# Plain float32 products in the first chunk's first four d_ff blocks of an attention + FFN kernel on one core

## The chip, the cores and the metric

One NeuronCore of a Trainium2 chip. The metric is device microseconds of one execution. Five engines run their own instruction streams, each in the order in which the program was built: TensorE (PE, with its weight loads as PEld), VectorE (DVE), ScalarE (ACT), GpSimd (POOL) and SyncE (SP, which issues all DMAs here). An instruction waits for semaphores of others, and everything behind it on its engine waits with it.

## What is computed

Attention over a sliding window with four sink keys, and behind it an FFN:

```python
scores = 0.125 * q @ k.T                         # batch 4, 8 heads, seq 768, head 64
keep = (pos_k < n_sink) | (0 <= pos_q - pos_k < window)    # 4 sinks, window 128
a = softmax(where(keep, scores, -1e9));  x = (a @ v)       # as 3072 tokens x 512
h = x @ w_in                                     # 512 x 2048
g = where(h >= 1, h, where(h <= -1, 0, (h + 1) ** 2 / 4))
out = g @ w_out                                  # 2048 x 512, float32
```

## The kernel before

The 3072 tokens are cut into eight chunks of 384 tokens (`CT` = 3 tiles of 128), the four first halves of the batches ahead of the four second halves. A **unit** is one head of one chunk; there are 64. For each unit `attn_steps(n)` issues scores (PE, L249), the row maximum (DVE, L253), the exponential (ACT, L257), a sum on POOL (L262), its reciprocal (DVE, L263), the normalisation (L275 on ACT, L277 on DVE), transposes (PE, L326 to L328), their copies (ACT, L329, L333), and the product with v. Scores of unit n stand beside transposes of unit n-1, and the product of an older one.

The first 16 units (`NATIVE`, chunks 0 and 1) take their operands in float32 itself: the PE multiplies them as they are, and two heads share one product with v (`av2`, L369, copied to `xn` by L371). All other products are made of float32r parts: an operand is rounded to float32r, the rest is a second part, and a product is three matmuls (high by high, high by low, low by high). Rounding is a cast on ACT, the rest a subtraction on DVE or POOL.

The FFN goes over 16 blocks j of 128 d_ff columns. `stage1` makes a block of h (four slices `ct` of d_model, three matmuls each, L445), then relu, square (ACT, L452, L453), a min/max (DVE, L454), the cast `gh` (ACT, L455) and the rest `gl` (L456, on POOL for chunk 0, else on DVE). `stage2` (L464) multiplies it with w_out, two blocks later (`LAG`).

The weights come as 64-bit words, 32 tiles of 0.5 MB (w_in and w_out of each block in turn, n = 0 to 31). `weights(n)` fetches up to `AHEAD` = 3 tiles beyond n, and `decode` turns one into float32 with three bit operations on DVE (L157 to L159), then splits it: a cast on ACT (L160) and a subtraction on DVE (L161).

The loop over chunks builds a **stretch** at a time: `spread` merges the attention steps of one chunk with the steps of what is due beside it. The **first stretch** is the attention of chunk 0 (up to the scores of unit 9) with the first `WFIRST` = 13 weight tiles. The **second stretch** is the rest of chunk 1's attention with the FFN of chunk 0 and the other 19 tiles. The third has the FFN of chunk 1, and so on. PE's order is the order written here; the other engines' orders were set by a scheduler when the program was built. All fetches of the first two stretches stand in one queue on SP, in program order.

## Time and profile before

| | |
|---|---|
| median of 3 runs | 725.88 us (724.31 to 726.3) |
| the profiled execution | 726.5 us, its span 724.8 us |
| busy PE / PEld / DVE / ACT / POOL | 97% / 85% / 73% / 70% / 42% |
| mean granted PE clock | 0.992 |
| instructions | 12264 |

Busy shares are of the span. A matmul's record holds its time in the pipeline, so consecutive records overlap; what one costs is read from start to start. DVE's and ACT's records overlap too, by about a tenth of a microsecond. "A <- B" after an idle time names what ended the wait.

### The profile page before, as it was taken

Reading aid. Unit: us, or ns where it says so; the run is one execution under the profiler, and the core shown is the slowest. Engines: PE = TensorE matmul, PEld = TensorE weight load, DVE = VectorE, ACT = ScalarE, POOL = GpSimd, SP = SyncE. Lnnn points to the kernel's source line nnn. Section 1 sums busy time; section 2 is a strip of 40 time slices with the busy share of each in tenths; the row PEclk is TensorE's granted clock in tenths of the full one; section 3 lists DMA queues with packets and bytes.
Section 4 is the critical chain, followed back from the end, with each engine's and each line's share of the span. In section 5 each row is a group of like instructions: output and inputs, shape, how many; then the busy total and the mean of one; then the engine's idle time right before and its main releaser. Section 6 shows DMA issues by size and latency. Waiting matters only on the chain.

```text
span 724.8 us, 12264 instructions
## 1 busy us (share of the span) xinstructions
PE 699.7 (97%) x3841; PEld 615.6 (85%) x3841; DVE 529.4 (73%) x1393; ACT 504.4 (70%) x1313; POOL 305.7 (42%) x529
## 2 busy tenths in 40 slices
PE   6879999999999999999999999999999999999996
PEld 4547778899989999999889998999989989989895
DVE  8988989578786777687887887878877787833221
ACT  5887677687776777687677877778777867644432
POOL 3002224755453545455564666645556365500000
PEclk9989999999999999999999999999999999999999
DMA  7453453222221322153242533334323342101001
GB/s 291 146 225 127 188 193 121 58 89 58 57 57 33 96 65 66 46 186 114 88 125 64 170 126 115 115 103 137 122 82 127 107 125 74 67 1 44 0 1 48
DMA packets 38568, 73.54 MB, mean 101 GB/s; under 512 B 6752, under 2 KB 21088, under 8 KB 38496
## 3 DMA queue, kind: packets, MB, share of 16 engines
q1 hardware_dynamic: 38496, 72.68, 31.2%
q8 instruction: 32, 0.52, 0.3%
q14 instruction: 40, 0.33, 0.1%
HBM read 66.37 MB, written 6.29 MB: 100 GB/s over the span
## 4 chain that ended last, share of the span: by engine, by line
PE 70%; DVE 13%; ACT 6%; DMA 5%; POOL 3%; issue 2%; POOLq 0%; ACTq 0%; SPq 0%; DVEq 0%
PE h_ps L445 28%; PE o_ps L464 28%; PE ps_a L249 6%; PE ps_a L404 4%; ACT p L257 2%; PE ps_a L336 2%; DVE k_s L233 2%; DMA k_r<-qk 1%; DVE p L277 1%; PE ps_a L369 1%; PE ps_a L326 1%; DMA r<-vx 1%; DVE gl L456 1%; ACT k_s L231 1%; DMA r<-qk 1%
## 5 line engine op out<-in xcount | busy, mean ns | idle before, releaser
L445 PE MATMUL h_ps<-x,wi 128*128 128x384 f32 x1536 | 310.1, 340 | 0.0
L445 PEld LDWEIGHTS h_ps<-x,wi 128*128 128x128 f32 x1536 | 262.7, 188 | 10.8 <-issue 2.7
L464 PE MATMUL o_ps<-w,gh 128*128 128x512 f32 x768 | 243.6, 398 | 0.0
L464 PE MATMUL o_ps<-w,gl 128*128 128x512 f32 x384 | 150.9, 393 | 0.3 <-POOL gl L456 0.3
L464 PEld LDWEIGHTS o_ps<-w,gh 128*128 128x128 f32 x768 | 134.1, 188 | 15.8 <-issue 1.4
L454 DVE SCALAR_TENSOR_TENSOR g<-g,h_ps 128x384 f32<-128x384 f32 x128 | 70.2, 548 | 66.4 <-ACT g L453 65.5
L452 ACT ACTIVATE g<-h_ps,half 128x384 f32<-128x384 f32 x128 | 73.9, 577 | 62.0 <-PE h_ps L445 61.6
L257 ACT ACTIVATE p<-p,peak 128x260 f32<-128x260 f32 (+1 forms) x192 | 94.0, 490 | 30.7 <-DVE peak L253 29.2
L235 POOL TENSOR_TENSOR q_l<-r,q_h 128x384 fp32r<-128x384 f32 x48 | 50.4, 1049 | 131.9 <-ACT q_h L234 121.6
L455 ACT CAST gh<-g 128x384 fp32r<-128x384 f32 x128 | 65.5, 511 | 53.0 <-DVE g L454 52.1
L456 DVE TENSOR_TENSOR gl<-g,gh 128x384 fp32r<-128x384 f32 x112 | 70.2, 627 | 24.7 <-ACT gh L455 23.7
L464 PEld LDWEIGHTS o_ps<-w,gl 128*128 128x128 f32 x384 | 72.0, 188 | 18.2 <-POOL gl L456 0.8
L253 DVE CUSTOM_DVE_ANT_0 p<-ps_a,m 128x260 f32<-128x260 f32 (+1 forms) x176 | 68.2, 398 | 16.6 <-PE ps_a L249 15.9
L233 DVE TENSOR_TENSOR k_s<-k_r,k_s 64x524 fp32r<-64x524 f32 (+1 forms) x44 | 47.2, 1073 | 42.8 <-ACT k_s L231 42.7
L453 ACT ACTIVATE g<-g 128x384 f32<-128x384 f32 x128 | 67.0, 524 | 2.6
L348 POOL TENSOR_SCALAR_AFFINE_SELECT pt<-pt 128x384 fp32r<-128x384 f32 (+1 forms) x96 | 50.3, 525 | 23.8 <-DVE pt L341 21.8
L277 DVE TENSOR_SCALAR p<-p,stat 128x132 f32<-128x132 f32 (+1 forms) x160 | 56.8, 404 | 0.2
L262 POOL TENSOR_SCALAR stat<-stat 128x3 f32<-128x3 f32 x64 | 28.6, 447 | 66.1 <-ACT p L257 61.4
L346 POOL TENSOR_SCALAR_AFFINE_SELECT pt<-pt 128x384 fp32r<-128x384 f32 (+1 forms) x96 | 52.6, 549 | 6.9 <-ACT pt L340 2.7
L404 PEld LDWEIGHTS ps_a<-pt,v_s 128*128 128x128 f32 x304 | 46.5, 188 | 2.2
L404 PE MATMUL ps_a<-pt,v_s 128*128 128x256 f32 (+1 forms) x304 | 46.4, 272 | 0.0
L249 PE MATMUL ps_a<-k_s,q_h 128*128 128x260 f32 (+1 forms) x144 | 40.4, 281 | 4.4 <-DVE sk L343 3.1
(116 smaller groups left out, 986.1 us busy)
## 6 DMA issues: line engine op xcount, KB each, us to landing
r<-qk SPq DMA_DIRECT2D x48, 192.0 KB
k_r<-qk SPq DMA_DIRECT2D x32, 262.0 KB
w<-w_in SPq DMA_DIRECT2D x16, 512.0 KB
w<-w_out SPq DMA_DIRECT2D x16, 512.0 KB
again<-w_in SPq DMA_DIRECT2D x16, 512.0 KB
...
```

The source lines that it names most:

```text
L249: nc.tensor.matmul(ps[:, lo:260], lhsT=q[:, i * P:(i + 1) * P], rhs=k_s[:, c0:c0 + 260 - lo], start=(j == 0), stop=(j == len(qs) - 1))
L253: found = nc.vector.tensor_tensor_reduce(out=p[:, i, lo:260], in0=ps[:, lo:260], in1=m, scale=-0.125, scalar=3.0e38, op0=ALU.add, op1=ALU. ...
L257: nc.scalar.activation(p[:, i, lo:260], p[:, i, lo:260], AF.Exp, bias=peak_i, scale=-1.0, accum_out=stat[:, i:i + 1])
L277: (nc.gpsimd if eng == "p" else nc.vector).tensor_scalar(p[:, i, lo:260], p[:, i, lo:260], r, None, op0=ALU.mult)
L404: nc.tensor.matmul(z, lhsT=w, rhs=y, start=(n == 0), stop=(n == len(mms) - 1))
L445: nc.tensor.matmul(h_ps[:, :T], lhsT=w_i[j][:, w, ct * P:(ct + 1) * P], rhs=x[:, y, ct], start=(ct == 0 and n == 0), stop=(ct == NCT - 1 a ...
L452: nc.scalar.activation(g, h_ps[:, :T], AF.Relu, bias=half, scale=0.5)
L453: nc.scalar.activation(g, g, AF.Square)
L454: nc.vector.scalar_tensor_tensor(g, g, 1.0, h_ps[:, :T], op0=ALU.min, op1=ALU.max)
L455: nc.scalar.copy(gh, g)
L456: (nc.gpsimd if row0 == GL_POOL else nc.vector).tensor_tensor(gl, g, gh.bitcast(F32), op=ALU.subtract)
L464: nc.tensor.matmul(o_ps[tt], lhsT=gg[:, tt * P:(tt + 1) * P], rhs=w_o[j][:, w], start=(j == 0 and n == 0), stop=(j == NJ - 1 and n == 2))
```

## The change

In chunk 0, blocks 0 to 3 (`PLAIN` = 4) are multiplied as float32 itself: one plain matmul stands where three float32r matmuls stood, in both stages, on the decoded weights, on `xn` and on an unsplit `gh`. So the first eight weight tiles are decoded without cast and subtraction; `halves(j)` splits them later, in the stretch of chunk 1, whose FFN takes its blocks in the order 4 to 15, 0 to 3. The first stretch has 10 weight tiles instead of 13, the second 22. `gl` of chunk 0 (12 blocks now) goes to DVE. Of the three normalisations of a unit, chunk 0 keeps one on DVE and two on ACT, and chunk 1 has all three on ACT. All weight tiles come from one pool of 33 buffers (before: 16 constants and a pool of 16), three tiles are fetched ahead to the end, q's tiles have two buffers instead of three, and the later second reading of the weights uses the spare buffer.

```diff
 NATIVE = 16
+PLAIN = 4
-GL_POOL = 0
-NORM = "vaa"
+NORM = ("vaa", "aaa")
-WFIRST = 13
+WFIRST = 10
...
+    def decode(w, o, words):
         low, x = words[:, :, 0], words[:, :, 1]
+        nc.vector.tensor_scalar(o, x, 3, 0x3FFFFFFF, op0=ALU.logical_shift_left, op1=ALU.bitwise_and)
+        nc.vector.scalar_tensor_tensor(o, x, -0x40000000, o, op0=ALU.bitwise_and, op1=ALU.bitwise_or)
+        nc.vector.scalar_tensor_tensor(w, low, 29, o, op0=ALU.logical_shift_right, op1=ALU.bitwise_or)
+
+    def parts(t, w):
+        nc.scalar.copy(t[:, 0], w)
+        nc.vector.tensor_tensor(t[:, 1], w, t[:, 0].bitcast(F32), op=ALU.subtract)
+
+    def halves(j):
+        w = plain.pop(j).bitcast(F32)
+        with tc.issue_after(last_max[-1].ins):
+            for i in (0, 1):
+                t = (w_i, w_o)[i][j] = wpool.tile([P, 2, DM], F32R, name="w")
+                parts(t, w[:, i])
...
-        for deep, late, f in ((3, 4, load2), (2, 1, values2)):
+        for deep, late, f in ((2, 2, load2), (2, 1, values2)):
...
+        if j in plain:
+            nc.tensor.matmul(h_ps[:, :T], lhsT=plain[j][:, 0, cs].bitcast(F32), rhs=xn[:, ct],
+                             start=(ct == 0), stop=(ct == NCT - 1))
+        else:
+            for n, (w, y) in enumerate(((0, 0), (0, 1), (1, 0))):
+                nc.tensor.matmul(h_ps[:, :T], lhsT=w_i[j][:, w, cs], rhs=x[:, y, ct],
+                                 start=(ct == 0 and n == 0), stop=(ct == NCT - 1 and n == 2))
...
+        if j in plain:
+            gh = gh.bitcast(F32)
+            nc.vector.scalar_tensor_tensor(gh, g, 1.0, h_ps[:, :T], op0=ALU.min, op1=ALU.max)
+            hs[j] = gh, None
+            return
...
-        (nc.gpsimd if row0 == GL_POOL else nc.vector).tensor_tensor(gl, g, gh.bitcast(F32), op=ALU.subtract)
+        nc.vector.tensor_tensor(gl, g, gh.bitcast(F32), op=ALU.subtract)
...
+        if j in plain:
+            terms = [(gh, plain[j][:, 1].bitcast(F32))]
+        else:
+            terms = [(gh, w_o[j][:, 0]), (gh, w_o[j][:, 1]), (gl, w_o[j][:, 0])]
...
+        js = [(j + PLAIN * (c == 1)) % NJ for j in range(NJ)]
...
+            if c == 1 and n % 2 and n // 2 in range(1, PLAIN + 1):
+                steps.append((0.0, lambda j=n // 2 - 1: halves(j)))
```

**PE, where the second stretch begins**, before: scores of units 10 and 11 (ps_a<-qp) stand singly among blocks 0 to 2 of stage 1.

```order
L249 MATMUL ps_a<-qp 128x128
L445 MATMUL h_ps<-x,wi_151 128x384 x3
L249 MATMUL ps_a<-qp 128x260
L445 MATMUL h_ps<-x,wi_151 128x384 x9
L249 MATMUL ps_a<-qp 128x260
L445 MATMUL h_ps<-x,wi_152 128x384 x3
L326 MATMUL ps_a<-ident,p 128x128 x2
L328 MATMUL ps_a<-ident,p 4x128
L445 MATMUL h_ps<-x,wi_152 128x384 x9
```

The same place of the change (L266, L463 and L343 are the lines of these steps there; `w` is a decoded weight tile):

```order
L266 MATMUL ps_a<-qp 128x128
L463 MATMUL h_ps<-xn,w 128x384
L266 MATMUL ps_a<-qp 128x260
L463 MATMUL h_ps<-xn,w 128x384 x3
L266 MATMUL ps_a<-qp 128x260
L463 MATMUL h_ps<-xn,w 128x384
L343 MATMUL ps_a<-ident,p 128x128 x2
L345 MATMUL ps_a<-ident,p 4x128
L463 MATMUL h_ps<-xn,w 128x384 x2
```

Each group of three became one, and everything up to block 3 is of the plain kind, attention included. Over the whole second stretch a run of plain matmuls is followed by float32r ones 22 times before, and 14 times now.

**DVE, at the first weight tiles of the first stretch** (o and w: decode; ISA: the row maximum of a unit), before:

```order
L253 ISA p,peak<-ps_a,m1n 128x260
L253 ISA peak 128x1
L263 RECIPROCAL stat<-stat 128x3
L277 TENSOR_SCALAR p<-p,stat 128x128
L157 TENSOR_SCALAR o<-w 128x512
L253 ISA p,peak<-ps_a,m_106 128x260
L253 ISA peak 128x1
L158 SCALAR_TENSOR_TENSOR o<-w,o 128x512
```

The change at that place:

```order
L156 TENSOR_SCALAR o<-w 128x512
L157 SCALAR_TENSOR_TENSOR o<-w,o 128x512
L270 ISA p,peak<-ps_a,m1n 128x260
L270 ISA peak 128x1
L280 RECIPROCAL stat<-stat 128x3
L158 SCALAR_TENSOR_TENSOR w<-w,o 128x512
L270 ISA p,peak<-ps_a,m_106 128x260
L270 ISA peak 128x1
```

The first decode begins two operations ahead of unit 1's second maximum and ahead of unit 0's reciprocal; the subtractions that follow further down before (L161) are gone for the first eight tiles.

**DVE, in the middle of the second stretch** before (L454 is the min/max of a block):

```order
L253 ISA p,peak<-ps_a,m_109 128x128
L253 ISA peak 128x1
L157 TENSOR_SCALAR o<-w 128x512
L161 TENSOR_TENSOR wi_158<-o,wi_158 128x512
L253 ISA p,peak<-ps_a,m1n 128x260
L253 ISA peak 128x1
L158 SCALAR_TENSOR_TENSOR o<-w,o 128x512
L159 SCALAR_TENSOR_TENSOR o<-w,o 128x512
```

And of the change (L483 is gl):

```order
L270 ISA p,peak<-ps_a,m_109 128x128
L270 ISA peak 128x1
L158 SCALAR_TENSOR_TENSOR o<-w,o 128x512
L156 TENSOR_SCALAR o<-w 128x512
L270 ISA p,peak<-ps_a,m1n 128x260
L270 ISA peak 128x1
L483 TENSOR_TENSOR gl<-g,gh 128x384
L157 SCALAR_TENSOR_TENSOR o<-w,o 128x512
L162 TENSOR_TENSOR w<-o,w 128x512
```

A gl stands between the maxima and the decodes, where before POOL had it.

## Rows read from the trace of the kernel before

**Rows 1.** The page: the span, and PE's busy tenths in 40 slices of 18.1 us.

```profile
span 724.8 us, 12264 instructions
PE   6879999999999999999999999999999999999996
```

**Rows 2.** Busy time in the three stretches from one product of a pair of heads to the next (us from the start; length, then busy us and instructions of PE, PEld, DVE, ACT, POOL, granted clock, DMA share, GB/s), and their sum.

```profile
33.60:43.80 10.20, 7.89 (x43) 4.97 (x41) 9.35 (x29) 8.84 (x27) 0.71 (x2) 0.83 0.62 219
sum 30.60, PE 23.63 PEld 14.90 DVE 27.94 ACT 26.87 POOL 1.62; mean PE 7.88 PEld 4.97 DVE 9.31 ACT 8.96 POOL 0.54
```

**Rows 3.** PE's timeline over one of them (start, us, what; the idle time before and what ended it).

```profile
33.53 1.38 PE L249 MATMUL ps_a<-qp 64*128 64x128 f32 x6
34.85 0.44 PE L326 MATMUL ps_a<-ident,p 128*128 128x128 f32 x2
...
36.58 1.14 PE L249 MATMUL ps_a<-qp 64*128 64x260 f32 x4 [0.29 <-ACT spn L333]
39.58 0.80 PE L326 MATMUL ps_a<-ident,p 128*128 128x128 f32 x2 [1.86 <-ACT p L275]
...
41.16 2.40 PE L369 MATMUL ps_a<-pt,v_s 128*64 128x128 f32 x12
...
43.75 0.93 PE L249 MATMUL ps_a<-qp 64*128 64x128 f32 x4
```

**Rows 4.** Groups of instructions from 23.4 to 54 us, ACT and DVE: the parts of the weights' decoding (count | busy us, mean ns | idle before).

```profile
L160 ACT CAST wi<-o 128x512 fp32r<-128x512 f32 x5 | 3.1, 615 | 0.8 <-DVE o L159 0.7
L160 ACT CAST w<-o 128x512 fp32r<-128x512 f32 x5 | 3.1, 611 | 0.0
L158 DVE SCALAR_TENSOR_TENSOR o<-w,o 128x512 int32<-128x512 int32 x8 | 5.5, 684 | 0.0
L161 DVE TENSOR_TENSOR wi<-o,wi 128x512 fp32r<-128x512 f32 x5 | 3.4, 688 | 2.0 <-ACT wi L160 2.0
L157 DVE TENSOR_SCALAR o<-w 128x512 int32<-128x512 int32 x8 | 3.3, 418 | 0.0
```

**Rows 5.** Two stretches of the same time, as in rows 2: the granted clock is the third number from the end.

```profile
33.30:40.10 6.80, 4.49 (x26) 2.70 (x23) 6.62 (x24) 6.20 (x20) 0.23 (x1) 1.00 0.80 279
40.10:43.50 3.40, 3.40 (x19) 2.27 (x21) 3.03 (x7) 2.35 (x8) 0.49 (x1) 0.50 0.24 99
```

**Rows 6.** PE's timeline in the first 24 us.

```profile
12.96 2.52 PE L249 MATMUL ps_a<-qp 64*128 64x128 f32 x6
15.41 0.69 PE L326 MATMUL ps_a<-ident,p 128*128 128x128 f32 x2
...
23.34 0.93 PE L249 MATMUL ps_a<-qp 64*128 64x128 f32 x4
```

**Rows 7.** PE's timeline where the second stretch begins.

```profile
54.41 0.80 PE L445 MATMUL h_ps<-x,wi 128*128 128x384 f32 x3
55.14 0.70 PE L249 MATMUL ps_a<-qp 64*128 64x260 f32 x2
55.77 1.84 PE L445 MATMUL h_ps<-x,wi 128*128 128x384 f32 x9
57.54 0.70 PE L249 MATMUL ps_a<-qp 64*128 64x260 f32 x2
```

**Rows 8.** PE's timeline late in the second stretch, with no attention between.

```profile
135.25 2.25 PE L445 MATMUL h_ps<-x,wi 128*128 128x384 f32 x12
137.33 0.63 PE L464 MATMUL o_ps<-w,gh 128*128 128x512 f32 x2
...
139.41 2.25 PE L445 MATMUL h_ps<-x,wi 128*128 128x384 f32 x12
```

**Rows 9.** The second stretch: for whom PE waited from 54 to 146 us (us, times, longest), and busy time in two parts of it.

```profile
PE o_ps L464 <- POOL gl L456: 0.3, 1, 0.3
...
54.00:132.00 78.00, 77.71 (x421) 60.43 (x420) 70.79 (x160) 56.93 (x151) 26.04 (x28) 1.00 0.43 150
132.00:146.00 14.00, 13.67 (x69) 11.89 (x68) 5.26 (x12) 7.95 (x20) 8.35 (x13) 1.00 0.19 52
```

**Rows 10.** Groups of instructions from 54 to 132 us, DVE and POOL.

```profile
L158 DVE SCALAR_TENSOR_TENSOR o<-w,o 128x512 int32<-128x512 int32 x19 | 16.8, 884 | 0.2
L159 DVE SCALAR_TENSOR_TENSOR o<-w,o 128x512 int32<-128x512 int32 x19 | 15.2, 801 | 0.0
L157 DVE TENSOR_SCALAR o<-w 128x512 int32<-128x512 int32 x19 | 9.4, 493 | 2.3 <-DMA w<-w_in 2.3
L456 POOL TENSOR_TENSOR gl<-g,gh 128x384 fp32r<-128x384 f32 x12 | 14.3, 1192 | 31.8 <-ACT gh L455 18.5 <-issue 13.1
L235 POOL TENSOR_TENSOR q_l<-r,q_h 128x384 fp32r<-128x384 f32 x3 | 4.2, 1387 | 0.2
```

**Rows 11.** One DVE and one POOL instruction of the timelines at 86 us.

```profile
86.88 1.49 DVE L161 TENSOR_TENSOR wi<-o,wi 128x512 fp32r<-128x512 f32 x1
...
86.59 1.23 POOL L456 TENSOR_TENSOR gl<-g,gh 128x384 fp32r<-128x384 f32 x1 [3.80 <-issue]
```

**Rows 12.** DVE's timeline: the end of w_in's last tile.

```profile
124.59 0.68 DVE L161 TENSOR_TENSOR wi<-o,wi 128x512 fp32r<-128x512 f32 x1
```

**Rows 13.** The page's group of gl on DVE in the other chunks, and the busy time of the third stretch.

```profile
L456 DVE TENSOR_TENSOR gl<-g,gh 128x384 fp32r<-128x384 f32 x112 | 70.2, 627 | 24.7 <-ACT gh L455 23.7
...
146.00:230.00 84.00, 84.00 (x482) 76.86 (x481) 64.79 (x182) 60.93 (x169) 40.32 (x74) 1.00 0.21 59
```

More of the change, by code (lines that the diff above doesn't have):

```diff
@@ L137, in attn_ffn @@
         nc.gpsimd.memset(t, 0.0)
-    w_i = [const.tile([P, 2, DM], F32R, name=f"wi{j}") for j in range(NJ)]
-    w_o = [None] * NJ
-    raw = {}
+    w_i, w_o = [None] * NJ, [None] * NJ
+    raw, plain = {}, {}
     inorder = [True]
@@ L168, in f @@
             j, i = n // 2, n % 2
-            for k in range(n, min(n + min(AHEAD, NJ - n // 2 - 1) + 1, 2 * NJ)):
+            for k in range(n, min(n + AHEAD + 1, 2 * NJ)):
                 if k not in raw:
@@ L172, in f @@
                     fetch(raw[k], (w_in, w_out)[k % 2][k // 2].bitcast(I32))
-            words = raw[n].rearrange("p (c two) -> p c two", two=2)
-            if i:
-                w_o[j] = wpool.tile([P, 2, DM], F32R, name="w")
-            with tc.issue_after(last_max[-1].ins) if last_max else nullcontext():
-                decode((w_i, w_o)[i][j], moe.tile([P, DM], I32, name="o"), words)
+            words = raw.pop(n).rearrange("p (c two) -> p c two", two=2)
+            raw[n] = None
+            if j < PLAIN:
+                if not i:
+                    plain[j] = wpool.tile([P, 2, DM], I32, name="w")
+            else:
+                t = (w_i, w_o)[i][j] = wpool.tile([P, 2, DM], F32R, name="w")
+            o = moe.tile([P, DM], I32, name="o")
+            with tc.issue_after(last_max[-1].ins) if last_max else nullcontext():
+                if j < PLAIN:
+                    decode(plain[j][:, i], o, words)
+                else:
+                    decode(o, o, words)
+                    parts(t, o.bitcast(F32))
         return f
@@ L272, in scores @@
             r = stat[:, CT + i:CT + i + 1]
-            eng = NORM[i] if units.index(u) < NATIVE else "v"
+            eng = NORM[units.index(u) // H][i] if units.index(u) < NATIVE else "v"
             if eng == "a":
@@ L422, in attn_steps @@
         if n == 0:
-            steps = [steps[i] for i in (0, 3, 1, 4, 2)]
+            steps = [steps[i] for i in (0, 2, 1, 3)]
         if n + 1 >= NATIVE and -1 in us:
@@ L443, in stage1 @@
         h_ps = hs[j]
-        for n, (w, y) in enumerate(((0, 0), (0, 1), (1, 0))):
-            nc.tensor.matmul(h_ps[:, :T], lhsT=w_i[j][:, w, ct * P:(ct + 1) * P], rhs=x[:, y, ct],
-                             start=(ct == 0 and n == 0), stop=(ct == NCT - 1 and n == 2))
+        cs = slice(ct * P, (ct + 1) * P)
+        if j in plain:
+            nc.tensor.matmul(h_ps[:, :T], lhsT=plain[j][:, 0, cs].bitcast(F32), rhs=xn[:, ct],
+                             start=(ct == 0), stop=(ct == NCT - 1))
+        else:
+            for n, (w, y) in enumerate(((0, 0), (0, 1), (1, 0))):
+                nc.tensor.matmul(h_ps[:, :T], lhsT=w_i[j][:, w, cs], rhs=x[:, y, ct],
+                                 start=(ct == 0 and n == 0), stop=(ct == NCT - 1 and n == 2))
         if ct < NCT - 1:
@@ L512, in attn_ffn @@
     early = ExitStack()
-    first.append(early.enter_context(tc.tile_pool(name="first", bufs=3)))
+    first.append(early.enter_context(tc.tile_pool(name="first", bufs=2)))
     prev = wsteps[:WFIRST]
@@ L525, in attn_ffn @@
             early.close()
-            chk.append(fast.enter_context(tc.tile_pool(name="chk", bufs=2)))
-        prev = moe_steps(rows[c], tail)
+            chk += [fast.enter_context(tc.tile_pool(name=f"chk{i}", bufs=i)) for i in (2, 1)]
+        prev = moe_steps(rows[c], tail, c)
         if c == 0:
@@ L549, in attn_ffn @@
     nc.vector.tensor_copy(other, flag[0:1, 2:3])
-    for _, f in prev + tail:
+    for _, f in prev + sum(tail, []):
         f()
@@ L629, in attn_ffn @@
                     tail = []
-                    for _, f in moe_steps(b * S + t0 * P, tail) + tail:
+                    for _, f in moe_steps(b * S + t0 * P, tail) + sum(tail, []):
                         f()
```

55 lines of the change are left out of this document (27 added, 28 removed).

## The prediction

> **What bounds the kernel now.** I read the page first: PE is busy in nearly the whole span, except in the first three slices [rows 1]. So a change can win time in the first 54 us or by taking work off PE; it loses time wherever it gives PE work or lets it wait. Then I read the first stretch in pieces. From one product of a pair of heads to the next takes 10.2 us, three times over, and there DVE is busy 9.31 us in the mean and ACT 8.96, PE 7.88 [rows 2]. PE's row shows where the pair's time goes: scores and transposes are done early, PE then stands for 1.86 us until ACT's normalisation frees the transposes at 39.58, and from there transposes and the product take until 43.75, 4.17 us [rows 3]. That last piece is slow because the granted clock had fallen to half, 1.2 GHz, after the sparse time before it, while it had been whole, 2.4 GHz, from 33.3 to 40.1 [rows 5]. The three score matmuls of a unit (six records) take 1.32 us there [rows 3] and 2.45 us from 12.96 to 15.41 [rows 6]: before the first product, PE runs at the lower level as well and is busy back to back, so nothing on DVE can shorten that piece.
>
> From 54 us on PE is the bound. In the second stretch it waited for one thing that the profile shows, 0.3 us for gl on POOL [rows 9]. DVE was busy 70.79 of 78.0 us to 132 and 5.26 of 14.0 us behind it [rows 9], but ahead of its need: w_in's last tile was done at 125.3 [rows 12] and first used at 139.41 [rows 8].
>
> **The change, part by part.** The sum is made against the profiled execution, 726.5 us (span 724.8 and 1.7 around it), which lies 0.6 above the median of 725.88.
>
> *The start.* The first decode now stands with two operations ahead of unit 1's second maximum and unit 0's reciprocal, 0.42 and 0.68 us long [rows 4]. PE is back to back soon behind it, so the delay stays: +0.3 us, between 0 and the two operations' 1.1.
>
> *The wait ahead of the transposes.* In each of the three pairs two weight casts stand ahead of the awaited normalisation on ACT, 0.6 us each [rows 4], and they go for the plain tiles. Three bit operations per unit stay in DVE's queue ahead of the reciprocals. Out of 1.2 us at most and 0 at least I take 0.7 a pair: -2.1 us.
>
> *The clock.* At the whole clock the transposes and the product would take half of 4.17 us, 2.1. With a shorter period PE's idle time is a larger part shorter, but 1.2 us of the 1.86 remain; so the clock may fall in some pairs and not in others. I take 1.7 of three pairs: -3.4 us, with 0 and -6.2 as bounds. The floor below everything is ACT: 26.87 us less 6.2 us of casts [rows 2, 4] leave 6.9 us a pair, that is 9.9 us off the three.
>
> *Plain products.* A unit's scores, 128 + 2 x 260 = 648 columns, take 1.32 us [rows 3], 2.04 ns a column with their two ends; the product with v, of 128 rows and with two heads side by side, takes 2.59 us for 768 columns at half the clock [rows 3], which is 1.69 ns at the whole. The new matmuls are wide, so I take 1.69: 0.65 us for 384 columns and 0.86 for 512. Three float32r matmuls take 2.08/4 = 0.52 us in stage 1 and 2.08/3 = 0.69 in stage 2 [rows 8]. There are 16 of the first and 12 of the second: 16 x 0.13 + 12 x 0.17 = +4.1 us; with 2.04 it is +8.4.
>
> The Trainium skill gives another price: its page Perfetto Trace Analysis, section Engine Utilization, puts TensorE's output rate for FP32_LOW_HIGH at half the normal one, two cycles a column. By it the new matmuls would take 0.32 and 0.43 us, and this term would be 16 x -0.20 + 12 x -0.26 = -6.3 us. The rows do not bear it out: each plain matmul shows as two records, and the pair of them takes four cycles a column.
>
> *Changes of kind.* A plain 260-column matmul between float32r ones takes 0.63 us [rows 7] where 260 x 1.69 ns are 0.44, and the float32r matmuls between two plain ones take 0.73 for three and 1.77 for nine [rows 7], 0.21 more than 0.173 each. So each such round costs 0.40 us. The second stretch has 22 of them before and 14 now: -3.2 us. The lower bound for this gain is 0, if plain matmuls pay the same ends among themselves.
>
> *DVE in the second stretch.* Three more tiles: 3 x (0.42 + 2 x 0.68 + 0.69) = +7.4 us; twelve gl at 0.627 us [rows 13] = +7.5; eight normalisations of 128 columns fewer, each below the 0.42 us of a decode's first operation, which is four times as wide [rows 4], so between 0 and -3.4: I take -2.2. Against that stands what POOL's gl did: while it ran, a DVE subtraction took 1.49 us [rows 11] instead of 0.69 [rows 4]. L158, L159 and L157 took 884, 801 and 493 ns there against 684, some 680 and 418 before 54 us [rows 4, 10]: 19 x (0.20 + 0.12 + 0.075) = 7.5 us, of which POOL's gl, 14.3 of 18.5 us [rows 10], made 5.8. In all DVE has +6.9 us: 83.0 busy of the 92 us instead of 76.1. PE still bounds, with the 14.1 us of lead as its cover. I allow +1.0 us for waits behind a fuller DVE; if the cover is gone, see the rivals.
>
> *The rest.* PE's wait for gl on POOL goes: -0.3. The later splits are eight casts and eight subtractions, 4.9 and 5.5 us, in a stretch where PE never waited, DVE was busy 64.79 and ACT 60.93 of 84.0 us [rows 13]; ACT's third normalisation goes into the second stretch, where it was busy 56.93 of 78.0 [rows 9]. I put both at 0; uncovered, the splits would cost 5.5. The fetches still stand behind the wait for a pair's v buffer on SP, before and now, and q's third buffer goes; but q of a pair is then asked for two units ahead, and the DMAs were busy to 0.24 and 0.80 of their time in a pair's two halves [rows 5], so 0 here too, 1 at most.
>
> Sum: +0.3 - 2.1 - 3.4 + 4.1 - 3.2 + 1.0 - 0.3 = -3.6, so 722.9 for an execution like the profiled one and **722.3 us** beside the median.
>
> **The rivals.**
> *The clock stays whole in all three pairs.* For it: the period shrinks towards ACT's 6.9 us and PE's share rises. Against it: a wait of 1.2 us or so remains, and in the pair shown the clock fell behind a wait of 1.86 us. It gives 2.8 more: 719.5.
> *The clock falls in each pair as before.* For it: the same order of work, and the wait in the same place. Then the 3.4 us don't come: 725.7.
> *DVE becomes the bound of the second stretch: slower.* For it: it is nearly full to 132 us already. If POOL's other work (q_l) keeps delaying the decodes as gl did, DVE has 70.8 + 7.4 + 7.5 - 1.7 (six of the normalisations) = 84.0 us to do in the time to 132, with 7.2 idle as now 91.2, 13.2 too many. Behind 132 it has 8.7 us free; if half of that makes up for it, PE waits 8.8 us instead of 1.0: 730.1. The point from which it decides is where the maxima and gl come later than PE's next step, that is, when DVE's delay passes the 14.1 us by which the weights are early. Against it: gl is gone from POOL.
> *Plain matmuls pay ends,* 2.04 ns a column: 4.3 more, 726.6.
> *Plain matmuls need two cycles a column,* as if the array passed the operands only twice: 10.4 less, 711.9. This is what the rule of the Trainium skill's page above would do here.
>
> **How the numbers follow.** The forecast has 0.45, the whole clock 0.13, the lost clock 0.20, DVE 0.12, ends 0.08, two cycles 0.02. The measurement tells 0.3%, 2.2 us, from no change. The forecast's own range is 720 to 725; three quarters of it lie below 723.7. So faster is 0.33 + 0.13 + 0.02 and a little of the lost clock, 0.50; slower is nearly all of DVE, 0.11; the same 0.39. The range reaches from ACT's side, 718.5, to 728, where part of DVE's case is left out.
>
> **What would show it.** The product of the fourth pair ends at 54.0 now; I expect 48.8 (46 with the whole clock, 52 without any). The pairs' periods fall from 10.2 to 8 or 9 us, with the granted clock at half in one or two. Plain matmuls of stage 1 start 0.65 us apart, of stage 2 0.86. From the end of the first stretch to the start of chunk 1's FFN it should take 1 to 2 us longer than before, PE without waits over 0.5 us. DVE's decode operations of the second stretch come down towards 0.68 us. The forecast is wrong if PE waits there for DVE, or if the first stretch ends after 52.

## The result and the profile after

The changed kernel is slower: 735.17 us, median of 4 (732.56 to 735.56), beside 726.09 us (724.31 to 728.62) of the kernel before in the same comparison; ratio 1.0115, 95% interval 1.0076 to 1.0153. The forecast was 722.3 us in a range of 718.5 to 728. The profiled execution took 735.5 us, 9.0 more than that of before. From the page of after (40 slices of the span, busy tenths; PEclk is the granted clock in tenths):

```profile
span 733.8 us, 12175 instructions
...
PE   6889998999999999999999999999999999999996
...
PEclk9999999899999999999999999999999999999998
```

Beside [rows 1] PE has one digit higher, in the third slice, and one lower, the 8 in the seventh (110 to 128 us), and the clock an 8 in the slice behind it. The page shows no more than that. Where the time went shows when the span is cut at the copies that end a stage. The copy of the fourth pair's product starts at 50.4 us instead of 54.1; the first chunk's first output copy at 157.7 instead of 152.6; the second chunk's at 239.9 instead of 233.4; the eighth's at 725.6 instead of 716.4. So the first stretch gave 3.7 us, the second took 8.8, the third took 1.4, the rest 2.7.

The three pairs of the first stretch (time, then busy time and instruction count of PE, PEld, DVE, ACT, POOL, the granted clock, DMA share, GB/s), which answer to [rows 2, 5]:

```profile
24.70:33.20 8.50, 6.63 (x41) 4.55 (x41) 6.45 (x23) 7.43 (x24) 0.69 (x2) 1.00 0.59 204
33.20:41.00 7.80, 6.80 (x44) 4.34 (x44) 6.57 (x24) 7.12 (x26) 0.45 (x2) 1.00 0.63 219
41.00:50.40 9.40, 7.27 (x38) 4.46 (x37) 6.43 (x22) 8.12 (x28) 0.45 (x2) 0.82 0.50 182
```

The periods are 8.5, 7.8 and 9.4 us instead of 10.2, with the clock whole in two of the three. For the second stretch, PE's waits from 50 to 136 us (engine, line, waited for; total, times, longest), which answer to [rows 9], and PE's own row where they lie:

```profile
PE ps_a L354 <- DVE sk L300: 1.8, 1, 1.8
PE ps_a L353 <- DVE p L294: 1.3, 1, 1.3
```

```profile
124.84 0.69 PE L467 MATMUL h_ps<-x,w 128*128 128x384 f32 x3
126.83 0.72 PE L353 MATMUL ps_a<-ident,p 128*128 128x128 f32 x3 [1.31 <-DVE p L294]
129.37 0.38 PE L354 MATMUL ps_a<-ident,sk 128*8 128x128 f32 x1 [1.82 <-DVE sk L300]
129.40 3.23 PE L467 MATMUL h_ps<-x,w 128*128 128x384 f32 x9
132.56 2.40 PE L386 MATMUL ps_a<-pt,v_s 128*64 128x128 f32 x12
...
135.26 0.73 PE L495 MATMUL o_ps<-w,gh 128*128 128x512 f32 x2
```

PE waits twice for unit 16, the first unit of chunk 2: for its normalised p, and for `sk`, the small copy of the sink columns. Behind the waits the granted clock is at the lower of its two levels, 1.2 GHz:

```profile
124.90:129.30 4.40, 1.34 (x7) 0.72 (x6) 4.40 (x15) 2.16 (x8) 2.31 (x3) 0.89 0.28 71
129.30:135.80 6.50, 6.43 (x28) 4.91 (x29) 6.47 (x15) 3.55 (x12) 4.21 (x7) 0.55 0.25 64
```

The pieces from 129.40 to 135.26 take 5.86 us; a product and nine stage-1 matmuls take 3.15 at the whole clock (rows of the run no_plain_glpool13 below). That is 2.7 us on top of 3.1 us of waits (a wait of 0.2 us for POOL, at 122 us, comes on top).

What VectorE did meanwhile (start, duration, line, operation). L270 with `p<-ps_a` is a maximum, L286, L280, L294 and L300 are unit 16's sum of columns, reciprocal, normalisation and `sk`; L156 to L158 and L162 decode weights:

```profile
121.07 0.41 DVE L270 CUSTOM_DVE_ANT_0 p<-ps_a,m 128x260 f32<-128x260 f32 x1
...
121.41 1.16 DVE L157 SCALAR_TENSOR_TENSOR o<-w,o 128x512 int32<-128x512 int32 x1
122.49 0.55 DVE L483 TENSOR_TENSOR gl<-g,gh 128x384 fp32r<-128x384 f32 x1
122.96 0.68 DVE L158 SCALAR_TENSOR_TENSOR o<-w,o 128x512 int32<-128x512 int32 x1
123.56 0.68 DVE L162 TENSOR_TENSOR w<-o,w 128x512 fp32r<-128x512 f32 x1
...
124.38 1.05 DVE L286 TENSOR_TENSOR p<-p 128x256 f32<-128x256 f32 x1
...
126.09 1.08 DVE L294 TENSOR_SCALAR p<-p,stat 128x128 f32<-128x128 f32 x3
127.09 0.68 DVE L157 SCALAR_TENSOR_TENSOR o<-w,o 128x512 int32<-128x512 int32 x1
127.69 0.68 DVE L162 TENSOR_TENSOR w<-o,w 128x512 fp32r<-128x512 f32 x1
128.29 0.54 DVE L481 SCALAR_TENSOR_TENSOR g<-g,h_ps 128x384 f32<-128x384 f32 x1
...
129.10 0.21 DVE L300 COPY sk<-p 128x8 f32<-128x8 f32 x1
```

From unit 16's last maximum to its `sk` are 8.0 us, in which six decoding instructions (one is in a gap of the rows), a gl, a min/max and three maxima of the next unit are done. The same place in the kernel before (L253 maximum, L269, L277, L283 for sum, normalisation and `sk`), and PE's use of `sk` there:

```profile
121.00 0.41 DVE L253 CUSTOM_DVE_ANT_0 p<-ps_a,m 128x260 f32<-128x260 f32 x1
...
121.35 1.15 DVE L159 SCALAR_TENSOR_TENSOR o<-w,o 128x512 int32<-128x512 int32 x1
122.43 1.23 DVE L269 TENSOR_TENSOR p<-p 128x256 f32<-128x256 f32 x1
...
123.99 0.68 DVE L277 TENSOR_SCALAR p<-p,stat 128x128 f32<-128x128 f32 x3
...
125.40 0.17 DVE L283 COPY sk<-p 128x8 f32<-128x8 f32 x1
...
126.71 0.27 PE L337 MATMUL ps_a<-ident,sk 128*8 128x128 f32 x1
```

Two decoding instructions (the other is that of [rows 12]) and one maximum, 4.4 us. There `sk` was ready at 125.6 and PE took it at 126.7: a lead of 1.1 us. Up to the copy of the eighth pair's product VectorE had 2.5 us more to do after the change, at a smaller share of a longer time. Before and after, with the 10 us in which PE waits:

```profile
54.00:132.70 78.70, 78.41 (x425) 61.13 (x424) 71.49 (x162) 57.35 (x152) 26.74 (x30) 1.00 0.43 149
120.00:130.00 10.00, 9.71 (x64) 8.11 (x64) 9.81 (x22) 8.10 (x25) 6.78 (x7) 1.00 0.31 95
```

```profile
50.40:135.40 85.00, 81.63 (x377) 55.30 (x378) 74.02 (x176) 59.60 (x160) 15.21 (x21) 0.96 0.46 166
120.00:130.00 10.00, 6.63 (x36) 5.39 (x35) 10.00 (x27) 7.73 (x23) 5.38 (x6) 0.92 0.27 72
```

From 120 to 130 us VectorE is full in both, 9.81 and 10.00 us. The busy share does not tell the kernel with the waits from the one without.

### The profile page after: what moved, and what is told of

Read it like the earlier page. It is cut to its first block, busy times and chain, and to the rows that moved or that the text cites. A ratio compares the mean times of both kernels' runs of the same rounds, so it can differ in the third digit from the quotient of the medians.

```text
span 733.8 us, 12175 instructions
## 1 busy us (share of the span) xinstructions
PE 706.3 (96%) x3813; PEld 613.2 (84%) x3813; DVE 529.5 (72%) x1397; ACT 507.0 (69%) x1317; POOL 289.1 (39%) x513
## 4 chain that ended last, share of the span: by engine, by line
PE 68%; DVE 14%; ACT 8%; DMA 4%; issue 2%; POOL 2%; SPq 0%; ACTq 0%; POOLq 0%
PE o_ps L495 27%; PE h_ps L467 26%; PE ps_a L266 5%; PE ps_a L421 3%; ACT p L274 2%; DVE p L294 2%; DVE k_s L250 2%; PE h_ps L463 2%; DVE gl L483 2%; PE ps_a L386 1%; DMA r<-qk 1%; PE ps_a L353 1%; DMA again<-w_out 1%; PE ps_a L343 1%; DVE p L286 1%
## 5 line engine op out<-in xcount | busy, mean ns | idle before, releaser
L467 PE MATMUL h_ps<-x,w 128*128 128x384 f32 x1488 | 302.7, 342 | 0.0
L467 PEld LDWEIGHTS h_ps<-x,w 128*128 128x128 f32 x1488 | 258.1, 189 | 10.1 <-issue 1.8
L495 PE MATMUL o_ps<-w,gh 128*128 128x512 f32 x768 | 247.4, 403 | 0.0
L495 PE MATMUL o_ps<-w,gl 128*128 128x512 f32 x372 | 146.8, 395 | 0.0
L481 DVE SCALAR_TENSOR_TENSOR g<-g,h_ps 128x384 f32<-128x384 f32 x124 | 68.0, 548 | 57.8 <-ACT g L474 56.9
L482 ACT CAST gh<-g 128x384 fp32r<-128x384 f32 x124 | 63.4, 512 | 51.7 <-DVE g L481 50.9
L483 DVE TENSOR_TENSOR gl<-g,gh 128x384 fp32r<-128x384 f32 x124 | 76.0, 613 | 29.3 <-ACT gh L482 28.5
L270 DVE CUSTOM_DVE_ANT_0 p<-ps_a,m 128x260 f32<-128x260 f32 (+1 forms) x176 | 68.3, 399 | 26.7 <-PE ps_a L266 25.7
L495 PEld LDWEIGHTS o_ps<-w,gl 128*128 128x128 f32 x372 | 69.8, 188 | 15.4
L250 DVE TENSOR_TENSOR k_s<-k_r,k_s 64x524 fp32r<-64x524 f32 (+1 forms) x44 | 45.7, 1039 | 40.1 <-ACT k_s L248 40.0
L294 DVE TENSOR_SCALAR p<-p,stat 128x132 f32<-128x132 f32 (+1 forms) x152 | 55.1, 415 | 0.1
L266 PE MATMUL ps_a<-k_s,q_h 128*128 128x260 f32 (+1 forms) x144 | 40.4, 280 | 5.1 <-DVE sk L360 3.9
```

The lines of the kernel that those rows point to most:

```text
L266: nc.tensor.matmul(ps[:, lo:260], lhsT=q[:, i * P:(i + 1) * P], rhs=k_s[:, c0:c0 + 260 - lo], start=(j == 0), stop=(j == len(qs) - 1))
L270: found = nc.vector.tensor_tensor_reduce(out=p[:, i, lo:260], in0=ps[:, lo:260], in1=m, scale=-0.125, scalar=3.0e38, op0=ALU.add, op1=ALU. ...
L294: (nc.gpsimd if eng == "p" else nc.vector).tensor_scalar(p[:, i, lo:260], p[:, i, lo:260], r, None, op0=ALU.mult)
L467: nc.tensor.matmul(h_ps[:, :T], lhsT=w_i[j][:, w, cs], rhs=x[:, y, ct], start=(ct == 0 and n == 0), stop=(ct == NCT - 1 and n == 2))
L481: nc.vector.scalar_tensor_tensor(g, g, 1.0, h_ps[:, :T], op0=ALU.min, op1=ALU.max)
L482: nc.scalar.copy(gh, g)
```

## The experiments

The table gives every run: tiles left for the second stretch, decoding instructions that stand in VectorE's queue between unit 16's last maximum and its `sk` (counted in the order of the built program), PE's listed waits from 54 to 160 us, the end of the first stretch, the time from there to the first output copy, and from that to the second chunk's. All but the medians and ratios come from one profiled execution each. The kernel before had medians of 725.6 to 727.8 us beside them. The end of the first stretch varies between executions: six of these traces (after, gl_on_pool, wlead60, wlead90 and the two with late loads) have the same order of instructions there, and it ends at 50.2 to 52.7.

| kernel | median us | ratio (95%) | tiles | decoding inside | waits | first stretch to | second | third |
|---|---|---|---|---|---|---|---|---|
| before | 726.1 | 1 | 19 | 2 | 0.6 | 54.1 | 98.5 | 80.8 |
| after | 735.2 | 1.0115 (1.0076 to 1.0153) | 22 | 6 | 3.3 | 50.4 | 107.3 | 82.2 |
| gl_on_pool | 737.9 | 1.0182 (1.0141 to 1.0223) | 22 | 7 | 5.6 | 50.3 | 108.3 | 82.5 |
| thirteen_first | 738.8 | 1.0180 (1.0139 to 1.0220) | 19 | 6 | 4.0 | 53.3 | 107.6 | 83.2 |
| no_plain | 735.6 | 1.0135 (1.0099 to 1.0171) | 22 | 7 | 4.3 | 54.8 | 103.5 | 82.2 |
| before_ten_gl | 740.2 | 1.0191 (1.0157 to 1.0226) | 22 | 7 | 11.2 | 53.4 | 113.2 | 82.8 |
| wlead60 | 736.6 | 1.0132 (1.0084 to 1.0181) | 22 | 6 | 4.5 | 50.6 | 105.8 | 83.3 |
| wlead90 | 743.0 | 1.0226 (1.0164 to 1.0287) | 22 | 6 | 6.0 | 52.7 | 111.6 | 82.3 |
| values_late | 737.0 | 1.0136 (1.0101 to 1.0171) | 22 | 8 | 5.8 | 50.0 | 109.6 | 83.2 |
| glpool13 | 733.9 | 1.0099 (1.0071 to 1.0127) | 19 | 6 | 1.4 | 54.8 | 102.7 | 82.5 |
| no_plain_glpool13 | 735.6 | 1.0136 (1.0106 to 1.0167) | 19 | 7 | 5.7 | 55.7 | 105.0 | 82.1 |
| before_ten_first | 734.3 | 1.0113 (1.0085 to 1.0141) | 22 | 7 | 6.2 | 54.1 | 106.7 | 81.0 |
| before_gl_dve | 728.8 | 1.0036 (1.0018 to 1.0054) | 19 | 4 | 0.8 | 54.1 | 98.9 | 82.6 |
| before_norm12 | 726.8 | 1.0007 (0.9992 to 1.0021) | 20 | 3 | 0.5 | 53.6 | 99.5 | 80.2 |
| thirteen_taper | 731.3 | 1.0058 (1.0030 to 1.0086) | 19 | 2 | 0 | 55.2 | 101.2 | 83.2 |
| no_plain_glpool13_taper | 728.8 | 1.0014 (1.0001 to 1.0028) | 19 | 3 | 0 | 56.9 | 98.4 | 81.2 |
| glpool13_taper | 732.5 | 1.0065 (1.0038 to 1.0092) | 19 | 2 | 0 | 55.0 | 100.6 | 83.5 |
| glpool11_taper | 735.3 | 1.0113 (1.0077 to 1.0148) | 21 | 3 | 2.6 | 52.3 | 105.0 | 83.6 |
| after_late_loads | 737.4 | 1.0153 (1.0121 to 1.0185) | 22 | 2 | 4.9 | 50.4 | 110.1 | 83.9 |
| gl_on_pool_late_loads | 736.7 | 1.0149 (1.0117 to 1.0182) | 22 | 3 | 3.6 | 50.2 | 108.1 | 83.6 |

### Is it VectorE's load, or the plain products?

gl_on_pool undoes one part of the change: `gl` of chunk 0 is subtracted on POOL.

```diff
-        nc.vector.tensor_tensor(gl, g, gh.bitcast(F32), op=ALU.subtract)
+        (nc.gpsimd if c == 0 else nc.vector).tensor_tensor(gl, g, gh.bitcast(F32), op=ALU.subtract)
```

> The changed kernel with one part undone: the gl of the first chunk's twelve split blocks is subtracted on POOL again, all else as changed. Theory A (VectorE is late at the end of the second stretch, and the two waits of 1.5 and 2.0 us and the half clock behind them are its doing): VectorE is relieved of 12 x 0.627 = 7.5 us, less what POOL's subtractions slow its decoding; the waits of PE for VectorE between 120 and 132 fall below 1 us together, the granted clock stays at 1.00 there, and the time falls by about 7 us, to 726.5 to 729.5. Theory B (the plain products and the changed order of the work cost the time, VectorE's load does not matter): the time stays within 1 us of the changed kernel's, 734 to 736.

Neither came: PE waited longer. VectorE's decoding from 100 to 135 us shows why the relief was none (count, busy us, mean ns), first in this run, then in the kernel after:

```profile
L162 DVE TENSOR_TENSOR w<-o,w 128x512 fp32r<-128x512 f32 x10 | 8.7, 872 | 0.0
...
L156 DVE TENSOR_SCALAR o<-w 128x512 int32<-128x512 int32 x8 | 6.4, 803 | 0.0
```

```profile
L162 DVE TENSOR_TENSOR w<-o,w 128x512 fp32r<-128x512 f32 x9 | 6.1, 683 | 0.4 <-ACT w L161 0.4
L156 DVE TENSOR_SCALAR o<-w 128x512 int32<-128x512 int32 x8 | 3.3, 412 | 0.0
```

While POOL subtracts, the same decoding takes longer, as [rows 11] showed. What was taken off VectorE came back in its other instructions: over the second stretch it was busy 85.9 us in both.

thirteen_first is the other half of the load:

```diff
-WFIRST = 10
+WFIRST = 13
```

> The changed kernel with thirteen tiles of weights in the first stretch instead of ten. Theory A: VectorE has 3 x 2.5 = 7.4 us less to do in the second stretch, PE does not wait for it between 115 and 132, the clock stays whole there, and the second stretch is 7 us shorter; the first stretch ends at 52 to 54.5 instead of 50.4 (as before, where it held thirteen); time 729.5 to 732. Theory B: the second stretch is as long as with ten, the first one longer, time 736 to 740.

Theory A's first stretch came, its second did not: 4.0 us of waits for the same two instructions and a granted clock of 0.66 from 130 to 140. So less load on VectorE, by either half, did not remove the waits.

no_plain leaves the plain blocks out (`PLAIN = 0`, and the first chunk's splits ahead of its products):

> The changed kernel without the part that gives it its name: no block is used in float32 itself, all sixteen are split ahead of the first chunk's products; ten tiles in the first stretch, gl on VectorE, ACT's normalization and the rest stay as changed. Theory A: VectorE has 4 more gl (2.5 us) in the second stretch, and 8 subtractions more in the first; PE's products are 4.1 us shorter and change kind more often (up to 3.2 us); the waits for VectorE ahead of 132 are at least as long as with plain blocks (3.5 us or more), and the clock halves behind them; time 733 to 739. Theory B (plain products are at fault): time 731 or less.

The time is that of theory A, but the waits are not: 3.8 of the 4.3 us are for POOL's `k_s` and `q_l` of unit 17, 0.5 for VectorE. The kernel is as slow without plain products, so they are not the main cause. The run also tells what they do in the first stretch. One of its pairs, and one of before_ten_first (below):

```profile
34.20:44.40 10.20, 7.90 (x41) 4.93 (x41) 7.35 (x25) 8.11 (x26) 0.45 (x2) 0.83 0.47 167
```

```profile
33.70:43.90 10.20, 7.90 (x41) 4.91 (x42) 7.35 (x25) 8.13 (x27) 0.46 (x2) 0.83 0.48 167
```

With ten tiles instead of thirteen VectorE has 2 us less to do in a pair than in [rows 2], and the pair still takes 10.2 us. Fewer tiles alone gave nothing. Plain tiles, which send no cast to ACT and no subtraction to VectorE, shortened the pairs, but only with fewer tiles: the seven kernels with ten tiles and plain blocks end the first stretch at 50.0 to 52.7 (eleven: 52.3), the four with thirteen tiles and plain blocks at 53.3 to 55.2, the kernel before at 54.1.

before_ten_gl puts the load on the kernel before:

```diff
-GL_POOL = 0
+GL_POOL = -1
...
-WFIRST = 13
+WFIRST = 10
```

> The kernel before with only what loads VectorE in the second stretch: ten tiles in the first stretch instead of thirteen (3 x 2.5 = 7.4 us), and all sixteen gl of the first chunk on VectorE (16 x 0.627 = 10.0 us, less 5.8 us that POOL's subtractions cost the decoding). No plain block. Theory A: PE waits 2 us or more for VectorE between 115 and 140, the granted clock falls there, and the time is 728 to 734 although the first stretch ends 2 to 4 us earlier. Theory B: no waits there, the first stretch's gain stays, time 721.5 to 725.

740 us, beyond theory A's range, with no plain block in it. The waits are for POOL's `k_s` there, 9.2 us in two. The two halves alone, in a later comparison:

> The kernel before with ten tiles in the first stretch instead of thirteen and nothing else. VectorE gets 3 x 2.5 = 7.4 us more in the second stretch. Theory A (VectorE has no room left there; what is queued ahead of unit 16's softmax decides): waits of 2 to 6 us between 110 and 135, half clock behind them, time 728 to 733. Theory L (the lead of 14 us that the prediction read covers 7.4 us): waits below 1 us, first stretch 1 to 3 us shorter, time 723 to 726.

> The kernel before with the first chunk's sixteen gl on VectorE and nothing else: 16 x 0.627 = 10.0 us more for VectorE, less up to 5.8 us of its decoding that POOL's subtractions held up. Theory A: waits of 1 to 4 us between 110 and 135, time 727 to 732. Theory L: no waits above 1 us, time within 1 us of before.

Ten tiles alone cost 1.1% and 6.2 us of waits, a little beyond theory A: theory L, which is the prediction's reading, is refuted, with no plain block and no other part of the change in the kernel. gl alone cost 0.4%, with 0.8 us of waits, which fits neither theory. The tiles weigh more.

### Can VectorE's work be moved in time?

```diff
-WLEAD = 0.75
+WLEAD = 0.6      # wlead60; 0.9 in wlead90
```

> The changed kernel with one number moved: the weights' steps are spread over the first 60% of the first chunk's feed-forward steps instead of the first 75%. Nothing is added or taken away on any engine; the decoding of the 22 tiles is only queued earlier. Theory A1 (what is late is the softmax of unit 16, the first of the third chunk, because its VectorE instructions are queued behind decoding and gl, and VectorE has been full since 100; VectorE has 9 us idle between 54 and 100 that could take three tiles): waits for VectorE between 115 and 132 fall from 3.1 us to below 1, clock whole, time 727 to 730. Theory A2 (VectorE's share of the second stretch is simply too large, wherever it is put): waits of 2 us or more, only earlier, time 733 to 737. Theory C (the order in which TensorE's steps stand gives the softmax of unit 16 too little time, whatever VectorE does): waits as in the changed kernel, 734 to 736.

> The same number moved the other way, to 90%: of the 22 tiles about three (7.4 us of VectorE) are decoded only behind the softmax of unit 16 instead of ahead of it. Theory A1 and A2: the waits for VectorE between 115 and 132 fall below 1 us and the clock stays whole there; a wait for the last weights (decoded about 15 us later) may come at 135 to 150 and take up to 3 us of it; time 727 to 732. Theory C: waits of 3 us at 125 to 130 as in the changed kernel, 734 to 736.

Both missed. With 0.6 PE waits 2.3 us for a maximum, 1.8 for `q_l` and `k_s` and 0.4 for `sk`, with the clock whole; with 0.9 the waits for `sk` and p stay at 2.6 us, and 2.4 more come for a block's gh and gl at 152 to 156 us. The number moves the decoding in the program, and the waits with it.

values_late asks for a pair's v one unit later, so that the weights behind it in SP's queue are not held up:

```diff
-        for deep, late, f in ((2, 2, load2), (2, 1, values2)):
+        for deep, late, f in ((2, 2, load2), (2, 0, values2)):
```

> The changed kernel with the loads of the pairs' values issued one unit later. In the trace these loads hold up the queue on SyncE for 41.8 us of the second stretch, three times, until TensorE has used the tile they overwrite, and the weights' loads stand behind them; the weights arrive in bursts at 50, 71 and 91. Theory D (VectorE is idle 9 us between 54 and 100 because weights arrive in bursts, and is overfull afterwards): weights flow evenly, VectorE's busy time between 54 and 100 rises from 37 to above 41 us, the waits at 125 to 132 fall below 1.5, time 727 to 731. Theories A1, A2 and C (the order of the queue is fixed by the program, VectorE waited only 0.3 us for weights there): no change above 1 us, 734 to 736.

VectorE was 39.8 us busy from 54 to 100 instead of 37.0, but the waits were 5.8 us. So the way these loads hold up the queue was not the cause.

### Both loads off, and the plain blocks off as well

glpool13 joins gl_on_pool and thirteen_first; no_plain_glpool13 takes the plain blocks out of it as well.

> The changed kernel with both loads taken off VectorE in the second stretch: thirteen tiles in the first stretch and the first chunk's twelve gl on POOL, as in the kernel before; the plain blocks and ACT's normalization stay. VectorE then has no more to do between 54 and 132 than in the kernel before (its 70.8 us, less 2.2 of normalization). Each of the two alone left the waits in place. Theory A (either sort, a sum that is over the limit with one of them still there): no waits for VectorE above 1 us ahead of 140, clock whole there; the first stretch ends at 53.3 as in the run with thirteen tiles, the plain products cost at most 4.1 us and give some 2.5 back in changes of kind; time 725 to 728. Theory C: waits of 3 us and half clock again, 734 to 738.

> The changed kernel with thirteen tiles in the first stretch and the first chunk's gl on POOL, and no plain block: beside the run glpool13 it differs by the plain blocks alone, beside the kernel before by ACT's normalization, the buffers and the order of the loads. It is to give the price of the plain products where no wait covers it. Theory P1 (as predicted: 4.1 us of products against 3.2 us saved in changes of kind): from the end of the first stretch to the first chunk's output 0.9 us less than in glpool13 (102.7), 101.8. Theory P2 (the plain products save next to nothing in changes of kind, because they change among themselves at the same price): 3 to 4.5 us less, 98.2 to 99.7, and a time of 726 to 729 with the first stretch at 54 to 55.

glpool13 lost the waits but for 1.4 us, and the clock stayed whole, and it was still 1% slower than before, between the two theories. no_plain_glpool13, with before's load and nothing plain, waited 5.7 us, and so gave no price of the plain products. PE's row in it, first a product and nine stage-1 matmuls at the whole clock, then two of the waits:

```profile
115.18 1.30 PE L386 MATMUL ps_a<-pt,v_s 128*64 128x128 f32 x12
...
116.63 1.86 PE L467 MATMUL h_ps<-x,w 128*128 128x384 f32 x9
118.33 0.63 PE L495 MATMUL o_ps<-w,gh 128*128 128x512 f32 x2
...
132.16 0.73 PE L353 MATMUL ps_a<-ident,p 128*128 128x128 f32 x3 [1.61 <-DVE p L294]
135.04 0.38 PE L354 MATMUL ps_a<-ident,sk 128*8 128x128 f32 x1 [2.15 <-DVE sk L300]
```

This run speaks against "VectorE's load" as the whole cause. The sharpest contrast with it is before_norm12, the kernel before with ACT's normalisation of the change and one tile fewer first:

> The kernel before with the one part of the change that relieves VectorE in the second stretch (all three normalizations of the second chunk's units on ACT: 8 x 0.28 = 2.2 us), and one tile fewer in the first stretch (2.5 us more in the second), so that VectorE's load there stays as it was. No plain block, gl on POOL. Theory A: no waits above 1 us in the second stretch, first stretch about 1 us shorter, time 724.5 to 726.5 beside 726 to 727 of the kernel before, that is the same or 1 to 2 us faster. Theory C (any disturbance of the order makes waits there): waits of 2 us or more, 728 to 732.

Same as before, 0.5 us of waits. So something else in the change makes waits. The table's column of decoding instructions points to it: in the runs so far 2 to 4 where PE hardly waits, 6 to 8 where it does, with glpool13 (6, and 1.4 us) between. The order of VectorE's queue was set when the program was built, and one expression of the change moves it.

### The order of VectorE's queue

The kernel before let the number of tiles fetched ahead fall towards the last tiles (a taper); the change keeps it at 3. Put back, alone, in thirteen_first, no_plain_glpool13 and glpool13:

```diff
-            for k in range(n, min(n + AHEAD + 1, 2 * NJ)):
+            for k in range(n, min(n + min(AHEAD, NJ - n // 2 - 1) + 1, 2 * NJ)):
```

> The run thirteen_first (thirteen tiles first, plain blocks, gl on VectorE) with one expression put back as it was before the change: the number of tiles loaded ahead falls from 3 towards the last tiles instead of staying 3. VectorE does the same work. In its fixed queue 2 decoding instructions instead of 6 then stand between unit 16's last maximum and its sk copy, and 8 instead of 6 behind it. Theory Q (the waits come from the decoding queued inside unit 16's softmax): waits for VectorE between 115 and 140 fall from 4.0 to below 1.5 us, clock whole, time 738.8 - 4 - 3.4 = 731, 729.5 to 733. Theory A (VectorE's load alone): waits stay, 737 to 740.

> The run no_plain_glpool13 (before's load: thirteen tiles first, gl on POOL, no plain block) with the same expression put back. Decoding inside unit 16's softmax: 3 instructions instead of 7. Theory Q: the 5.7 us of waits go and the clock stays whole, time 725.5 to 728.5. Theory A: it had no more load than before in the first place, so the cause is elsewhere, 734 to 737.

> The run glpool13 (thirteen tiles first, gl on POOL, plain blocks) with the same expression put back; decoding inside unit 16's softmax 2 instead of 6. It had 1.4 us of waits and whole clock there. Theory Q: waits below 0.7 us, time 731.5 to 733.5. Beside no_plain_glpool13_taper it gives the price of the plain blocks without waits: theory P1 (as predicted) up to 1 us more, theory P2 (changes of kind give next to nothing back) 3 to 4.5 us more from the end of the first stretch to the first chunk's output, less what the plain blocks save in the first stretch.

VectorE's work is the same, and 738.8 became 731.3 us, as theory Q said to 0.4 us. The stretch from 120 to 140 in thirteen_first and in thirteen_taper:

```profile
120.00:130.00 10.00, 8.88 (x52) 7.79 (x50) 9.97 (x22) 7.58 (x24) 5.70 (x6) 1.00 0.26 72
130.00:140.00 10.00, 7.10 (x33) 5.23 (x34) 6.74 (x18) 6.78 (x18) 4.82 (x9) 0.66 0.19 53
```

```profile
120.00:130.00 10.00, 10.00 (x59) 9.11 (x59) 9.24 (x28) 7.34 (x21) 2.55 (x3) 1.00 0.15 42
130.00:140.00 10.00, 10.00 (x61) 8.46 (x60) 8.19 (x19) 9.27 (x24) 6.94 (x10) 1.00 0.13 34
```

No waits are left, PE is busy throughout, the clock is whole. glpool13, which had had 1.4 us of waits, lost those and came to 732.5 us; without plain blocks 735.6 became 728.8, 0.3 above theory Q's range. In each of the three pairs PE's order is the same from end to end, and the other engines' orders differ only from about 107 us on. So for 19 tiles it is shown that the order of the queues makes the waits, and that the missing taper set it. The decoding inside unit 16's softmax is what the rows show of it; that its number alone decides is not shown, since glpool13 with six waited 1.4 us where thirteen_first with six waited 4.0, and ACT's and POOL's orders and the fetches moved too.

Two runs without waits also price the plain blocks, glpool13_taper and no_plain_glpool13_taper: 100.6 against 98.4 us in the second stretch, +2.2, which lies between P1 and P2. In the third they took 83.5 and 81.2, of which 1.3 is a wait of PE for an `sk`.

For 21 and 22 tiles the same recipe failed:

> The run glpool13_taper with eleven tiles in the first stretch instead of thirteen: VectorE has 5 us more in the second stretch, but its queue holds only 3 decoding instructions inside unit 16's softmax. Theory Q: waits below 1.5 us, first stretch 2 to 3 us shorter (51 to 52.5), time 728 to 730.5. Theory A: waits of 3 us or more and half clock, 733 to 738.

The time, 735.3, is in theory A's range, but PE waited 2.6 us, 2.0 of it for POOL's `k_s` and `q_l`, and the clock stayed whole, so neither theory fits.

after_late_loads and gl_on_pool_late_loads keep decoding out of unit 16's softmax by fetching nothing ahead for the last six tiles:

```diff
-            for k in range(n, min(n + AHEAD + 1, 2 * NJ)):
+            for k in range(n, min(n + (AHEAD if n < 26 else 0) + 1, 2 * NJ)):
```

> The changed kernel, with tiles 26 to 31 of the weights loading nothing ahead (the last three loads are issued at their own turn). VectorE's work is the same; between unit 16's last maximum and its sk copy stand 2 decoding instructions instead of 6, and 15 instead of 10 behind it. Theory Q: the waits of 3.1 us and the half clock behind them go, which is 7.2 us of the second stretch; up to 2 us may come back as waits for the last weights at 135 to 150; time 728 to 730. Theory A (22 tiles and twelve gl are more than VectorE can do there): waits of 2 us or more in another place of 115 to 150, time 732 to 736.

> The same, with the first chunk's gl on POOL (the run gl_on_pool, 737.9, with the late loads): 3 decoding instructions inside unit 16's softmax instead of 7. Theory Q: the 5.6 us of waits and the half clock go, time 728 to 731. Theory A: VectorE is held up by POOL instead of its own gl, waits of 2 us or more, 733 to 738.

The waits for unit 16's softmax went, and in after_late_loads these came instead:

```profile
PE ps_a L266 <- POOL k_s L250: 3.8, 1, 3.8
PE ps_a L266 <- POOL q_l L252: 1.1, 1, 1.1
```

They are for the next unit's keys and queries; gl_on_pool_late_loads waited 3.1 us for the same two and 0.5 for a maximum. In all ten kernels with 22 tiles PE waited 3.3 to 11.2 us in this stretch, whichever way the queue was ordered. Theory A had waits in another place, and they came, with a time beyond its range (737.4 against 732 to 736). That VectorE's load is their cause is not shown: in after_late_loads POOL itself waited for ACT's casts of `k_s` and `q_h`. The taper alone was not put back into the changed kernel with its 22 tiles; before_ten_first has the taper, and still seven decoding instructions inside. Whether some order of 22 tiles exists without waits is open.

## Why the prediction was wrong

**The step that failed** is the term *DVE in the second stretch*, +1.0 us "with its 14.1 us of lead as its cover". The lead was read from the weights: w_in's last tile was ready 14.1 us before its use. But the weights were never what PE waited for. In the same queue stands unit 16's softmax, whose `sk` had 1.1 us of lead before the change. Decoding that is early by 14 us delays the instruction behind it, which is not early at all. before_ten_first, with 7.4 us more decoding and nothing else changed, waited 6.2 us (2.2 for VectorE, 4.0 for POOL): the 14.1 us did not cover it. What the prediction gave as its sign of being wrong, PE waiting for DVE there, is what came. The rival *DVE becomes the bound* named the right engine, but its point of decision, the 14.1 us, was wrong in the same way, its chance of 0.12 rested on it, and it put 8.8 us of waits where 3.1 came. The sum of VectorE's work was too high if anything, +6.9 us against some +4.5 (81.3 us before and 85.9 after in the whole second stretch), and it could not tell where PE would wait.

**The clock behind a wait** was in the sum for the first stretch only. In the second it added 2.7 us to 3.1 us of waits.

**Plain products and changes of kind:** forecast +4.1 - 3.2 = +0.9; measured without waits +2.2. The price of a column held nearly (below: 2.04 us for three matmuls, against 3 x 0.65), but the gain from fewer changes of kind was too large. Counted as for the 22 and 14 (transposes left out), glpool13_taper has 15 rounds in the second stretch and its partner without plain blocks 22, which at 0.40 us would be -2.8 and a sum of +1.3. The rows of after, where everything up to 73 us is plain, show what was wrong:

```profile
52.20 2.20 PE L463 MATMUL h_ps<-xn,w 128*128 128x384 f32 x6
54.34 0.70 PE L266 MATMUL ps_a<-qp 64*128 64x260 f32 x2
54.97 0.91 PE L463 MATMUL h_ps<-xn,w 128*128 128x384 f32 x2
...
68.59 2.20 PE L463 MATMUL h_ps<-xn,w 128*128 128x384 f32 x6
70.63 1.88 PE L495 MATMUL o_ps<-w,gh 128*128 128x512 f32 x4
```

A score of 260 columns takes 0.63 us between plain matmuls too (54.34 to 54.97), as between float32r ones in [rows 7], and three plain matmuls ahead of it take 2.14, 0.19 more than 3 x 0.65. So plain matmuls pay such ends among themselves, which the forecast had as the lower bound of this gain and, as *Plain matmuls pay ends*, among its rivals. What then gave back the 1.9 us between +4.1 and +2.2 was not taken apart. The trace of after has the 14 rounds that the forecast counted. Two cycles a column did not come: three plain matmuls of stage 1, six records, take 2.04 us (68.59 to 70.63).

**The first stretch** was right in its mechanism and 1.5 us too good. The pairs gained 4.9 us against 5.5 expected, and the clock was whole in two of three, expected 1.7. The start lost 1.2 instead of 0.3; in the other five traces with the same order there it lost between nothing and 1.2, so this is no fixed price. Ten tiles without plain blocks (before_ten_first, no_plain) gained nothing, nor did plain blocks with thirteen tiles; whether it is ACT's casts or VectorE's subtractions that count was not taken apart.

**The rest at 0:** the third stretch took 1.4 us longer, 82.2 us, and PE waited 0.2 us of them. no_plain, which has no later splits, took 82.2 as well, so they are not shown to cost anything in after. Over all runs the third stretch took 80.2 to 82.8 us in the eight kernels without plain blocks, 82.2 to 83.9 in the twelve with them. The 2.7 us behind it stay open: from the second chunk's output to the last, all twenty kernels lie between 481.5 and 485.7 us in no clear order, before at 483.0 and after at 485.7.

Forecast (-3.6) and profiled execution (+9.0) are 12.6 us apart: 1.5 from the first stretch, 7.2 from the second, 3.9 behind it. Of the 7.2, some 2.0 are waits beyond the forecast's (+2.7 against +0.7), 2.7 the clock behind them, and 1.3 the plain products, if they cost here what they cost without waits; about 1 stays open. No run beat the kernel before; before_norm12 is equal to it.
